# Two chunks of the second sequence take turns in layer one, and preparation work changes its place

## The chip, the core and the metric

The kernel runs on one core of one Trainium2 chip. The metric is device time in microseconds (us); lower is better. The core's engines run side by side, each with its own queue that it takes in order: TensorE (PE) multiplies matrices and loads their stationary side (PEld), VectorE (DVE), ScalarE (ACT) and GpSimd (POOL) do elementwise work, and SyncE (SP) issues the DMA transfers. Engines wait for each other by semaphores.

## The reference

Attention with a narrow window and block summaries, then two feed-forward parts, all in fp32:

```python
# 2 sequences, 8 heads, 768 positions, head size 64; block 32, window 16
k_sum = k.reshape(B, H, nb, block, D).max(axis=3)
v_sum = v.reshape(B, H, nb, block, D).mean(axis=3)
scores_l = where(|i - j| < 16, scale * q @ k.T, -1e9)
scores_s = scale * q @ k_sum.T + log(block)
attn = softmax(concat(scores_l, scores_s)) @ concat(v, v_sum)

x = attn as [1536 tokens, 512]
h = maximum(maximum(x @ w1, x @ w2), x @ w3)      # 512 -> 768
x = h @ w_out                                     # 768 -> 512
y = (x @ w_a) * (x @ w_b)                         # 512 -> 1536, twice
out = y @ w_out2                                  # 1536 -> 512
```

## The kernel before

**Work.** The 1536 tokens are four chunks of 384: chunks 0 and 1 are the first sequence, 2 and 3 the second. Attention goes by groups, one pair of heads in one chunk: eight groups per sequence, groups 0 to 3 for its first chunk and 4 to 7 for its second. A group has scores on PE (`ps`, L187), an exponential on ACT (L191), the reciprocal of the sum on DVE (`r`, L199), the normalization on POOL (`s`, L201), transposes on PE (`pst`, copied to `aT`), value products on PE (`psv`) and a split into two parts that gives `x`. `steps` (L233) is the generator that hands this out in 44 steps per sequence.

**Layers.** Every dense product is three matmuls on split operands (`mm3`, L362). `layers12(c)` (L374) is a generator of 22 turns for chunk `c`: 18 turns of layer one (`ph`, 12 matmuls each; the three weight sets are joined by a maximum on evacuation, then split into `hg`) and 4 turns of layer two (`py`, 18 matmuls each). Layer three (`layer3`, L461; PSUM tiles `qb`, `qg`, `qd`) multiplies by `w_a` and `w_b` with Strassen's seven products for each sequence; its operands `yt` are splits of sums and differences (`yd`) of the layer-two results, made by `sums_of` (L424). Layer four is `po` (L520).

**Weights.** All 60 weight tiles of 512 KB lie in HBM as 64-bit numbers. Each is loaded (`w_load`), rounded to fp32 on ACT, DVE and POOL (`w_round`, L300 to L306) and split (`w_split`, `w_parts`, L310 and L311). The first 24 (N12) serve layers one and two, the other 36 layers three and four. `weights(most)` (L335) moves the three stages on, if buffers have room by its count and, from weight 24 on, once `gate` has been set.

**Order.** SP's queue keeps the program's order. On the other engines a scheduler orders by its own estimate of when operations are ready; `tc.issue_after(ins)` forces what the block traces on the engine of `ins` behind `ins` in that engine's queue. `last[0]` is the last group's reciprocal (DVE), `mark[0]` the latest evacuation by DVE in layer one. The bottom of the program (L559 to L583) first walks through the first attention's steps and calls `weights` at some of them (`PRE`), then goes through the string `turns`, a digit per turn that names the chunk, with the second attention's steps strewn in between the turns that `TURNS` names, and at last through layers three and four.

## Time and profile before

| | before |
|---|---|
| time, median of 3 runs | 590.12 us (588.95 to 592.65) |
| the profiled execution: time, span | 591.21 us, 589.3 us |
| PE busy | 551.3 us (94%) |
| DVE busy | 377.8 us (64%) |
| ACT busy | 278.7 us (47%) |
| POOL busy | 208.2 us (35%) |
| TensorE clock granted, mean | 0.982 |

The profile is one execution. The span runs from its first instruction to its last; the profiled execution's own time is 1.9 us longer. Busy is the time in which an engine has an instruction; matmuls overlap one another, so a busy PE need not be at its full pace. [...] The chain of work that ended last is 63% PE, 14% DVE, 7% DMA, 5% POOL and 5% ACT.

### The profile page before, as it was taken

What the parts mean: (1) busy time and instruction counts of PE and PEld (TensorE: products, weight loads), DVE (VectorE), ACT (ScalarE), POOL (GpSimd) and SP (SyncE); (2) the same over time, 40 slices, a digit from 0 to 9 for tenths busy, and PEclk for the clock granted to TensorE, in tenths of its full rate; (3) what the DMA queues carried; (4) which work ended last, traced back from release to release, by engine and by line L of the source; (5) the groups of instructions that cost most, each with busy time, mean ns of one, the idle gap of its engine ahead of it and who ended that gap; (6) DMA issues with size and microseconds to landing.
All of it is one profiled execution on the core that took longest, in us unless ns stands there. A gap on an engine that the chain in (4) does not pass through costs nothing.

```text
span 589.3 us, 8831 instructions
## 1 busy us (share of the span) xinstructions
PE 551.3 (94%) x3272; PEld 513.3 (87%) x3272; DVE 377.8 (64%) x780; ACT 278.7 (47%) x667; POOL 208.2 (35%) x184
## 2 busy tenths in 40 slices
PE   4778999999999999998889899999999999999997
PEld 3567989999999999997888789999999989999985
DVE  4786398857213331249998775777696796883374
ACT  3777657444434332246675565653543544331220
POOL 0497269943001221035652433332341351330030
PEclk9959999999999999999999999999999999999999
DMA  9998035933211000052121123122212212000005
GB/s 265 344 273 247 36 110 190 298 73 107 63 47 48 1 1 1 1 222 85 52 72 43 66 72 108 37 72 72 71 41 77 98 37 72 2 1 0 1 17 198
DMA packets 31291, 53.32 MB, mean 90 GB/s; under 512 B 2448, under 2 KB 18832, under 8 KB 31248
## 3 DMA queue, kind: packets, MB, share of 16 engines
q1 hardware_dynamic: 31248, 52.75, 28.2%
q8 instruction: 26, 0.43, 0.3%
q14 instruction: 17, 0.14, 0.1%
HBM read 49.59 MB, written 3.15 MB: 89 GB/s over the span
## 4 chain that ended last, share of the span: by engine, by line
PE 63%; DVE 14%; DMA 7%; issue 5%; POOL 5%; ACT 5%; SPq 1%; POOLq 0%; ACTq 0%; DVEq 0%
PE ph L365 15%; PE qb L365 13%; PE py L365 7%; PE qg L365 5%; PE po L529 5%; DMA w<-wall 5%; PE po L527 5%; PE po L528 5%; POOL w L306 3%; DVE wt L311 3%; PE qd L365 3%; PE ps L187 2%; PE psv L228 2%; DVE hg L369 2%; DVE w L305 2%
## 5 line engine op out<-in xcount | busy, mean ns | idle before, releaser
L365 PE MATMUL ph<-x,wt 128*128 128x384 f32 x864 | 164.2, 343 | 3.8 <-DVE nm L190 2.0
L365 PEld LDWEIGHTS ph<-x,wt 128*128 128x128 f32 x864 | 150.7, 191 | 5.3 <-ACT wt L310 2.2
L306 POOL TENSOR_TENSOR w<-w,w 128x512 int32<-128x512 int32 x60 | 86.7, 1450 | 122.6 <-DVE w L305 73.5
L365 PE MATMUL qb<-yt,wt 128*128 128x384 f32 x576 | 114.2, 339 | 7.3 <-DVE t L496 2.0
L365 PEld LDWEIGHTS qb<-yt,wt 128*128 128x128 f32 x576 | 101.6, 188 | 14.0 <-DVE t L496 3.2
L368 ACT ACTIVATE hg<-t 128x384 fp32r<-128x384 f32 x72 | 36.9, 521 | 81.0 <-DVE t L392 36.0
L499 POOL TENSOR_TENSOR t<-t,ca 128x384 f32<-128x384 f32 x36 | 42.8, 1204 | 88.4 <-DVE t L498 85.7
L365 PE MATMUL qg<-yt,wt 128*128 128x384 f32 x288 | 59.4, 339 | 1.4 <-DVE t L498 0.6
L539 DVE TENSOR_TENSOR acc<-po,acc 128x512 f32<-128x512 f32 x60 | 40.8, 687 | 26.9 <-PE po L529 26.7
L527 PE MATMUL po<-wt,hg 128*128 128x512 f32 x144 | 56.4, 392 | 0.5 <-ACT hg L368 0.5
L528 PE MATMUL po<-wt,hg 128*128 128x512 f32 x144 | 56.5, 393 | 0.0
L529 PE MATMUL po<-wt,hg 128*128 128x512 f32 x144 | 55.8, 395 | 0.2 <-DVE hg L369 0.2
L365 PE MATMUL py<-hg,wt 128*128 128x384 f32 x288 | 55.1, 341 | 0.3 <-ACT hg L368 0.3
L365 PEld LDWEIGHTS qg<-yt,wt 128*128 128x128 f32 x288 | 50.9, 189 | 4.1 <-DVE t L498 0.9
L191 ACT ACTIVATE s<-s,nm 128x120 f32<-128x120 f32 x96 | 37.1, 388 | 33.3 <-DVE nm L190 32.9
L365 PEld LDWEIGHTS py<-hg,wt 128*128 128x128 f32 x288 | 49.6, 188 | 0.8 <-ACT hg L368 0.6
L392 DVE TENSOR_TENSOR t<-ph,t 128x384 f32<-128x384 f32 x48 | 26.3, 552 | 36.0 <-PE ph L365 31.6
L369 POOL TENSOR_TENSOR hg<-t,hg 128x384 fp32r<-128x384 f32 x24 | 26.8, 1116 | 61.8 <-ACT hg L368 61.8
L187 PE MATMUL ps<-kept,q 128*128 128x120 f32 x192 | 38.3, 319 | 10.6 <-DVE kept L133 7.7
L311 DVE TENSOR_TENSOR wt<-w,wt 128x512 fp32r<-128x512 f32 (+1 forms) x44 | 35.2, 799 | 20.0 <-ACT wt L310 20.0
L190 DVE CUSTOM_DVE_ANT_0 s<-ps,kept 128x120 f32<-128x120 f32 x96 | 24.6, 278 | 36.0 <-PE ps L187 35.4
L310 ACT ACTIVATE wt<-w 128x512 fp32r<-128x512 f32 (+1 forms) x60 | 35.0, 583 | 25.0 <-POOL w L306 12.6
(72 smaller groups left out, 789.1 us busy)
## 6 DMA issues: line engine op xcount, KB each, us to landing
w<-wall SPq DMA_DIRECT2D x60, 512.0 KB, 3.4
q<-qt SPq DMA_DIRECT2D x16, 384.0 KB, 7.2
kept<-kt SPq DMA_DIRECT2D x8, 448.0 KB, 6.9
full<-vt SPq DMA_DIRECT2D x8, 384.0 KB, 6.2
out<-acc SPq DMA_DIRECT2D x12, 256.0 KB, 2.0
v<-vwin SPq DMA_DIRECT2D x16, 144.0 KB, 5.4
v<-vwin SPq DMA_DIRECT2D x16, 96.0 KB, 5.7
v<-vwin SPq DMA_DIRECT2D x16, 48.0 KB, 6.7
```

What stands on the lines that cost most here:

```text
L187: T.matmul(ps[:, a], q[:, i, a], k_t[p][:, k0:k0 + NC], start=True, stop=True)
L191: A.activation(s[:, a], s[:, a], AF.Exp, bias=nm[:, a:a + 1], scale=-1.0, accum_out=sm[:, a:a + 1])
L306: G.tensor_tensor(w.bitcast(I32), w.bitcast(I32), lw.bitcast(I32), ALU.add)
L311: eng.tensor_tensor(w[:, 1], r, w[:, 0], ALU.subtract)
L365: T.matmul(ps, w[:, i, o:o + P], x[:, j], start=first and n == 0, stop=last and n == 2, skip_group_check=more)
L368: A.activation(dst[:, 0], src, AF.Copy)
L369: eng.tensor_tensor(dst[:, 1], src, dst[:, 0], ALU.subtract)
L499: G.tensor_tensor(t, t, cs[c, f], ALU.mult)
L527: T.matmul(ps, g[:, 0], w[:, 0], start=(f == 0), stop=False)
L528: T.matmul(ps, g[:, 0], w[:, 1], start=False, stop=False)
L529: T.matmul(ps, g[:, 1], w[:, 0], start=False, stop=(f == 1))
L539: V.tensor_tensor(acc[c, i], ps, acc[c, i], ALU.add)
```

## The change

- `PRE` goes from (9, 4) to (18, 5): in the first attention `weights` is called at step 18 and every fifth after it, where it was at step 12 and every fourth; six weights instead of eight are started there. On DVE these are queued behind a group's reciprocal.
- `turns` was six turns of chunk 0, twelve pairs of chunks 0 and 1, six of chunk 1, four of layer two each, then all 22 of chunk 2 and all 22 of chunk 3. The first 44 stay. Then come eight turns of chunk 2, ten pairs of chunks 2 and 3, the four layer-two turns of chunk 2 and the last twelve of chunk 3.
- The second attention's steps go into turns 20 to 44 (were: 24 to 60).
- `gate` is set by chunk 2's fourth `hg` tile (was: chunk 3's second), and `fits` lets the later weights start once chunk 3 has done nine turns of layer one (was: fifteen), with ten tiles at most as before. From chunk 2 on one weight is started per turn (was: two), behind the latest evacuations on DVE and on ACT.
- The first sequence's sums are traced at turns 58, 62, 66 and 70, behind those evacuations. They were traced at chunk 3's layer two and held back by one-element POOL copies that read `hg`; those copies are gone.
- The first six of the later weights are rounded through PSUM, as the first 24 are.

```diff
@@ -55,7 +55,11 @@
 W64, W32, WBUFS, QB, SM, GB, BANKS = (6, 3), (4, 3), (24, 10), 3, 2, (12, 9), (2, 2, 1, 2, 2)
-AHEAD, PRE, TURNS = (4, 1), (9, 4), (6, (24, 42), (42, 60))
+GATE, ROOM, SUMS, EARLY34 = (2, 3), 16, (58, 62, 66, 70), 6
+AHEAD, PRE, TURNS = (4, 1), (18, 5), ((6, N1 - 6, 6, 4, 4, 8, N1 - 8, 4, 12), (20, 32), (32, 44))
@@ -291,7 +295,7 @@
         r = w64_t.pop(q).bitcast(U32).rearrange("p (n t) -> p n t", t=2)
         lw, hw = r[:, :, 0], r[:, :, 1]
         to = hw.bitcast(F32)
-        if q < N12:
+        if q < N12 + EARLY34:
             to = ps_c.tile([P, 512], F32, tag="c", name="psw")
         if BIAS_DVE[era(q)][q % 3]:
@@ -332,11 +336,15 @@
     w_at, w_done, w_freed, w_room = [0, 0, 0], 0, 0, 0
+    def fits(n):
+        return n <= N12 or n - w_freed <= ROOM and n - max(N12, w_freed) <= WBUFS[1]
     def weights(most):
         nonlocal w_done, w_room
         for _ in range(most):
-            if w_done == len(seq) or w_room + room[w_done] > w_freed + WBUFS[w_done >= N12] or w_done == N12 and not gate:
+            if w_done == len(seq) or not fits(w_room + room[w_done]) or w_done == N12 and not gate:
                 return
             w_room += room[w_done]
             w_done += 1
@@ -369,7 +377,7 @@
         eng.tensor_tensor(dst[:, 1], src, dst[:, 0], ALU.subtract)
-    ys, gate, mark = {}, [], [None]
+    ys, gate, mark = {}, [], [None, None]
     def layers12(c):
@@ -387,12 +395,12 @@
             def evac(f=f, m=m, ps=ps, ht=hs[f]):
                 prev, pend[0] = pend[0], temp(f"t{m}", c)
                 if m == 0:
-                    A.activation(pend[0], ps, AF.Copy)
+                    mark[1] = A.activation(pend[0], ps, AF.Copy).ins
                 else:
                     mark[0] = V.tensor_tensor(pend[0], ps, prev, ALU.max).ins
                     if m == 2:
                         split(ht, pend[0], G)
-                        if lastc and f == 1:
+                        if c == GATE[0] and f == GATE[1]:
                             gate.append(ht[:, 0, 0:1])
             late.append(evac)
@@ -400,8 +408,6 @@
             yield
         ys[c] = y_p.tile([P, 4, MAXT * P], F32, tag="y", name="y", bufs=NCH)
         for m in range(4):
-            if lastc:
-                sums_of(m // 2, m % 2 * 2 + 1, [hs[f][:, 0, 0:1] for f in (2, 3, 4, 5)])
             ps = bank("py")[:, 0:n_]
             for f in range(N2):
                 if m == 0 and f == N2 - 1:
@@ -421,23 +427,18 @@
         if c >= 2 and m % 2:
             sums_of(c, m)
-    def sums_of(c, m, behind=None):
+    def sums_of(c, m):
         b, j = divmod(c, 2)
         (b11, b21), (b12, b22) = ((y[:, 0:2], y[:, 2:4]) for y in (ys[2 * b], ys[2 * b + j]))
         def op(name, src):
             ops[b, name] = t = t_p.tile([P, 2, 2, MAXT * P], F32R, tag=name, name="yt")
-            if behind is not None:
-                G.tensor_copy(t[:, 0, 0, 0:1], behind[m])
             A.activation(t[:, 0], src, AF.Copy)
             V.tensor_tensor(t[:, 1], src, t[:, 0], ALU.subtract)
         def diff(tag, x, y):
             t = y_p.tile([P, 2, MAXT * P], F32, tag=tag, name="yd")
-            if behind is not None:
-                G.tensor_copy(t[:, 0, 0:1], behind[m])
             V.tensor_tensor(t, x, y, ALU.subtract)
             return t
@@ -556,20 +557,33 @@
             q += 2
-    for i in range(2):
-        V.memset(vpad[i], 0.0)
+    for x in vpad:
+        V.memset(x, 0.0)
     for n, _ in enumerate(steps(0)):
-        weights(1 if n >= PRE[0] and n % PRE[1] == 0 else 0)
-    turns = TURNS[0] * "0" + (N1 - TURNS[0]) * "01" + TURNS[0] * "1" + "00001111" + (N1 + 4) * "2" + (N1 + 4) * "3"
+        if n >= PRE[0] and (n - PRE[0]) % PRE[1] == 0:
+            with tc.issue_after(behind):
+                weights(1)
+        else:
+            behind = last[0]
+    turns = "".join(x * y for x, y in zip(TURNS[0], ("0", "01", "1", "0", "1", "2", "23", "2", "3")))
     behind = last[0]
     dense, todo, done = [layers12(c) for c in range(NCH)], steps(1), 0
     for i, c in enumerate(turns):
         next(dense[int(c)])
-        with tc.issue_after(behind):
-            weights(2 if c > "1" else 1)
+        if c < "2":
+            with tc.issue_after(behind):
+                weights(1)
+        if c > "1":
+            with tc.issue_after(mark[0]), tc.issue_after(mark[1]):
+                weights(1)
+                if i in SUMS:
+                    m = SUMS.index(i)
+                    sums_of(m // 2, m % 2 * 2 + 1)
         due = sum(min(1, max(0, i + 1 - i0) / (i1 - i0)) for i0, i1 in TURNS[1:])
         while done < int((STEPS * NP + 2) * due + 1e-6):
```

What the scheduler makes of it, at three places. The first is PE's queue at the end of the first attention (`ps`, `pst`, `psv` are scores, transposes and value products of groups 5 to 7; `ph` is layer one). Before:

```order
L365 MATMUL ph<-x,wt 128x384 x10
L211 MATMUL pst<-kept,s 120x128 x6
L187 MATMUL ps<-kept,q_107 128x120 x2
L365 MATMUL ph<-x,wt 128x384 x12
L228 MATMUL psv<-aT,v_111 64x64 x12
L211 MATMUL pst<-kept,s 120x128 x6
L365 MATMUL ph<-x,wt 128x384 x12
L228 MATMUL psv<-aT,v_112 64x64 x12
L365 MATMUL ph<-x,wt 128x384 x210
```

and with the change:

```order
L373 MATMUL ph<-x,wt 128x384 x11
L191 MATMUL ps<-kept,q_107 128x120 x2
L215 MATMUL pst<-kept,s 120x128 x6
L232 MATMUL psv<-aT,v_111 64x64 x12
L373 MATMUL ph<-x,wt 128x384
L215 MATMUL pst<-kept,s 120x128 x6
L373 MATMUL ph<-x,wt 128x384 x11
L232 MATMUL psv<-aT,v_112 64x64 x12
L373 MATMUL ph<-x,wt 128x384 x204
```

The first attention's last value products now stand behind 60 matmuls of layer one; before, they stood behind 114.

The second is ACT's queue in groups 2 and 3 (`s,sm` are exponentials; L300 and L302 or, with the change, L304 and L306 round a weight, L310 or L314 split it; `r` is the sum of group 2). Before, with the first weight's two operations and two exponentials just ahead of these rows:

```order
L368 ACTIVATE x<-psv 128x384
L302 ACTIVATE w_304<-w_304 128x512
L150 ACTIVATE v_111<-psvs 24x3x128 x2
L300 ACTIVATE psw<-w_306 128x512
L302 ACTIVATE w_306<-w_306 128x512
L191 ACTIVATE s,sm<-s,nm 128x120 x2
L310 ACTIVATE wt<-w_315 128x512
L302 ACTIVATE w_308<-w_308 128x512
L191 ACTIVATE s,sm<-s,nm 128x120 x2
L302 ACTIVATE w_310<-w_310 128x512
L300 ACTIVATE psw<-w_308 128x512
L191 ACTIVATE s,sm<-s,nm 128x120 x2
```

(the next row is `r`), and with the change, from the first weight on:

```order
L304 ACTIVATE psw<-w_385 128x512
L306 ACTIVATE w_385<-w_385 128x512
L195 ACTIVATE s,sm<-s,nm 128x120 x2
L306 ACTIVATE w_387<-w_387 128x512
L195 ACTIVATE s,sm<-s,nm 128x120 x2
L154 ACTIVATE v_111<-psvs 24x3x128 x2
L195 ACTIVATE s,sm<-s,nm 128x120 x2
L202 ACTIVATE r<-sm 128x6
L306 ACTIVATE w_389<-w_389 128x512
L195 ACTIVATE s,sm<-s,nm 128x120 x2
L306 ACTIVATE w_391<-w_391 128x512
L306 ACTIVATE w_393<-w_393 128x512
```

From the first weight to `r` nine weight operations stood in the queue; now three do, and the landing of the fifth weight (`w_393`) stands ahead of group 3's `r`. The sixth weight's first operation stands a few rows further on, ahead of group 4's exponentials. On POOL the normalizations of groups 2 and 3 now follow each other ahead of all weight work; before, six weight operations stood ahead of the first of them.

The third is DVE's queue where the later weights begin (`t` are evacuations of layer one, `w` and `wt` weights, `yd` and `yt` the first sequence's differences and splits). Before:

```order
L392 TENSOR_TENSOR t_2785<-ph,t_2769 128x384
L304 TENSOR_SCALAR w_2916<-w_2912 128x512
L329 TENSOR_TENSOR s<-w_2827,s 128x256
L311 TENSOR_TENSOR wt<-s,wt 128x512
L305 SCALAR_TENSOR_TENSOR w_2916<-w_2912,w_2916 128x512
L304 TENSOR_SCALAR w_3082<-w_3078 128x512
L441 TENSOR_TENSOR yd<-y 128x768
L305 SCALAR_TENSOR_TENSOR w_3082<-w_3078,w_3082 128x512
L311 TENSOR_TENSOR wt<-s,wt 128x512
```

and with the change, where the first two of these weights begin:

```order
L442 TENSOR_TENSOR yd<-y 128x768
L438 TENSOR_TENSOR yt<-yd,yt 128x768
L400 TENSOR_TENSOR t_2613<-ph,t_2578 128x384
L400 TENSOR_TENSOR t_2628<-ph,t_2598 128x384
L308 TENSOR_SCALAR w_2639<-psw 128x512
L308 TENSOR_SCALAR w_2646<-psw 128x512
L309 SCALAR_TENSOR_TENSOR w_2639<-psw,w_2639 128x512
L309 SCALAR_TENSOR_TENSOR w_2646<-psw,w_2646 128x512
L400 TENSOR_TENSOR t_2666<-ph,t_2613 128x384
L442 TENSOR_TENSOR yd<-y,yd 128x768
```

The first sequence's sums stood behind the first weights of layer three; now four of their eleven operations stand ahead of those weights and the rest among the first operations on them. The second sequence's first two splits (chunk 2's) now follow the first two weights, where they stood ahead of all.

## Rows read from the trace of the kernel before

**Rows 1.** Page, busy tenths of 40 slices of 14.7 us.
```profile
PE   4778999999999999998889899999999999999997
...
DVE  4786398857213331249998775777696796883374
```

**Rows 2.** Stretches: us, busy us (x instructions) per engine, granted clock, DMA share, GB/s.
```profile
0.00:60.00 60.00, 40.09 (x268) 33.20 (x268) 39.47 (x130) 40.21 (x126) 32.21 (x35) 0.86 0.93 283
60.00:120.00 60.00, 58.53 (x405) 56.68 (x402) 45.20 (x88) 36.22 (x86) 43.09 (x34) 1.00 0.54 158
120.00:195.00 75.00, 74.91 (x552) 72.38 (x551) 29.80 (x114) 30.87 (x108) 15.62 (x17) 1.00 0.21 60
195.00:255.00 60.00, 60.00 (x409) 58.62 (x409) 16.85 (x50) 17.06 (x48) 9.37 (x9) 1.00 0.00 1
255.00:345.00 90.00, 79.42 (x427) 74.73 (x427) 77.85 (x117) 53.74 (x100) 42.00 (x39) 0.98 0.26 94
345.00:570.00 225.00, 222.70 (x1152) 204.98 (x1151) 156.93 (x266) 98.63 (x198) 63.04 (x51) 1.00 0.14 47
```

**Rows 3.** Timeline of PE: start us, us, what, [idle before <-releaser].
```profile
30.30 0.69 PE L365 MATMUL ph<-x,wt 128*128 128x384 f32 x1 [2.05 <-DVE nm L190]
...
82.89 36.73 PE L365 MATMUL ph<-x,wt 128*128 128x384 f32 x210 [0.59 <-ACT x L368]
```

**Rows 4.** Waits of PE, 255 to 345 us: total us, times, longest us.
```profile
PE qd L365 <- DVE yt L435: 1.6, 1, 1.6
...
PE qb L365 <- ACT yt L434: 1.6, 2, 1.2
PE qd L365 <- ACT yt L434: 1.6, 1, 1.6
```

**Rows 5.** Groups of ACT, 15 to 60 us: busy us, mean ns | idle before, releaser.
```profile
L191 ACT ACTIVATE s<-s,nm 128x120 f32<-128x120 f32 x28 | 10.8, 388 | 0.3 <-DVE nm L190 0.2
L302 ACT ACTIVATE w<-w 128x512 int32<-128x512 uint32 x13 | 8.7, 668 | 4.5 <-DMA w<-wall 4.5
```

**Rows 6.** Timeline of SP's DMA issues.
```profile
17.31 3.97 SPq L286 DMA_DIRECT2D w<-wall  x5
```

**Rows 7.** Timeline of ACT, first weight and group 2's sum.
```profile
23.86 0.64 ACT L300 ACTIVATE psw<-w 128x512 f32<-128x512 f32 x1 [0.86 <-DMA w<-wall]
...
33.35 0.20 ACT L198 ACTIVATE r<-sm 128x6 f32<-128x6 f32 x1
```

**Rows 8.** Stretches of 15 us in the first attention, as rows 2.
```profile
15.00:30.00 15.00, 10.31 (x86) 8.78 (x86) 11.86 (x45) 11.80 (x37) 6.93 (x11) 0.96 1.07 344
30.00:45.00 15.00, 11.78 (x58) 9.65 (x59) 11.88 (x32) 11.84 (x35) 15.00 (x13) 0.50 0.90 262
45.00:60.00 15.00, 11.88 (x105) 10.03 (x103) 8.63 (x33) 11.24 (x38) 9.86 (x8) 0.97 0.84 264
```

**Rows 9.** Timeline of POOL: normalizations of groups 2, 4 and 7.
```profile
37.19 1.85 POOL L201 TENSOR_TENSOR s<-s,r 128x720 f32<-128x720 f32 x1
...
52.72 1.38 POOL L201 TENSOR_TENSOR s<-s,r 128x720 f32<-128x720 f32 x1
...
76.08 1.39 POOL L201 TENSOR_TENSOR s<-s,r 128x720 f32<-128x720 f32 x1 [4.22 <-DVE r L199]
```

**Rows 10.** Groups of DVE, 240 to 360 us, as rows 5.
```profile
L435 DVE TENSOR_TENSOR yt<-yd,yt 128x768 fp32r<-128x768 f32 x8 | 8.4, 1051 | 0.0
...
L441 DVE TENSOR_TENSOR yd<-y 128x768 f32<-128x768 f32 x4 | 4.5, 1120 | 1.2 <-POOL yd L440 1.2
```

**Rows 11.** Timeline: first load for layer three (SP), its first matmul (PE).
```profile
255.66 90.81 SPq L286 DMA_DIRECT2D w<-wall  x17
...
275.23 0.62 PE L365 MATMUL qb<-yt,wt 128*128 128x384 f32 x2 [1.17 <-ACT yt L434]
```

**Rows 12.** Waits of PE, 0 to 60 us.
```profile
PE pst L211 <- POOL s L201: 2.1, 2, 1.4
PE psv L228 <- ACT aT L215: 2.1, 2, 1.3
```

## The prediction

> **What bounds the kernel now.** I read the slices of the page first, then busy time by stage, then TensorE's own rows. In the slices [rows 1] TensorE (PE) is at 9 nearly everywhere, with two dents: the first 60 us, and a shallow one from about 255 to 345 us, where VectorE (DVE) stands at 9 in many slices instead. A busy PE overstates the work, because matmuls overlap: 210 in a row from 82.89 us took 36.73 us [rows 3], 0.1745 us each. So I count the matmuls of a stretch and multiply.
>
> From 120 to 255 us PE is busy 134.9 of 135 us, and from 345 to 570 us 222.7 of 225 [rows 2]: nothing to win there, and something to lose. From 255 to 345 us it ran 427 matmuls [rows 2]: 427 x 0.1745 = 74.5 us, and 0.3 more for six wider ones of layer 4, so 15.2 of 90 us are lost. DVE was busy 77.9 us in the same stretch, more than PE had work. PE stood idle there for 90 - 79.4 = 10.6 us; at least 4.8 of these ended with `yt`, the sums' operands, on DVE or ScalarE (ACT) [rows 4].
>
> In the first 60 us PE is idle for 20 us while DMA is at 0.93 of its time [rows 2]: attention inputs and the first weights come together. ACT takes its queue in order, and that holds both kinds of work; one weight operation alone (L302) found 4.5 us of weights that had not landed [rows 5].
>
> **The change: the start.** I measure it by one state: first attention complete, PE free for dense work. Before, this is at 82.9 us [rows 3] with 114 matmuls of layer one done. After, PE's queue has 60 at that place. The missing 54 cost 54 x 0.1745 = 9.4 us later. If the first attention ends at T, the start gains 82.9 - (T + 9.4) - S, with S a wait for the next weight.
>
> T goes group by group (a group is one pair of heads in one chunk; its normalization on POOL, `s`, is the mark I follow).
> - The first five weights are issued behind the last values of chunk 0 instead of ahead of them, 672 KB later. Before they were issued from 17.31 us [rows 6] and ACT had the first at 23.86 [rows 7]. At 262 to 344 GB/s [rows 8] 672 KB are 2.0 to 2.6 us, so the first lands at about 26.2, and the fifth at about 33.5 (512 KB are 1.5 to 2.0 us).
> - Between ACT's first weight and the sum `r` of group 2, three weight operations stand in its queue where nine stood. Six at about 0.6 us (0.668 less the overlap, [rows 5]) are 3.6 us; a split and two scores that now go ahead are 1.1 more; the first weight is 2.3 later. `r` goes from 33.35 [rows 7] to 31 or 32.
> - On POOL `s` of groups 2 and 3 now stand ahead of all weight work. Before, the first of them began at 37.19 [rows 9], after queued weight work. After: near 32, and near 34.6 for group 3, whose `r` stands behind the fifth weight's landing.
> - Group 4: ACT has the sixth weight ahead of its first score. Its 512 KB follow 672 KB of inputs, so it lands near 38. Sixteen ACT operations later (8 scores of 0.388 us, 8 others of 0.2 to 0.67, [rows 5], 7 us in all) `s` of group 4 starts near 45; before at 52.72 [rows 9].
> - Groups 5 to 7: before, `s` of group 7 came at 76.08 [rows 9], so 7.8 us a group. After, less weight work stands between, but each group has a weight's landing ahead of it on ACT, and 11 to 14 matmuls of layer one ahead of its transposes on PE. The floor is what ACT itself does in a group: six scores, three weight operations [rows 5] and some small ones, 4.5 us; with a tail of 3.5 us, T = 45 + 13.5 + 3.5 = 62. The ceiling is the old spacing and the old tail (76.08 to 82.89): 45 + 23.4 + 6.8 = 75.2, say T = 76. I take 5.6 us a group, since waits on weights get fewer but do not go, and 5 us for the tail: T = 67.
>
> The sixth weight's DVE work is queued behind the last reciprocal, so PE waits about S = 2 us for it. Gain: 82.9 - 76.4 - 2 = 4.5 us; bounds +9.5 (T = 62) and -4.5 (T = 76). From there layer one asks for a new weight every two turns (4.2 us), the pace that 60 to 120 us had, where PE was busy 58.5 of 60 us and POOL 43.1 [rows 2]: no further loss.
>
> **The change: the middle.** The second attention's steps go from turns 24 to 60 into turns 20 to 44. PE's own work is the same, and PE is what is full there. DVE's 29.8 and ACT's 30.9 of 75 us [rows 2] leave room for half as much again. Chunk 3's first turn now comes right behind the last value product, so PE waits once for a split, as it does for 0.59 us at 82.89 [rows 3]. I take 1 us lost, bounds 0 and 4.
>
> **The change: from layer one to layer three.** Two things leave the stretch that DVE fills. The first sequence's sums (7 splits and 4 differences of 1.05 to 1.12 us, [rows 10], 12 us of DVE) go to turns 58 to 70; DVE was busy 16.9 of 60 us there [rows 2], which hides them. Without that cover they cost what they cost now. The 11 one-element POOL copies go, for which DVE waited 1.2 us [rows 10]. And the next layers' weights are loaded from about turn 60 and worked from turn 69. Before, their first load was at 255.66 us and layer three's first matmul 19.6 us later, behind `yt` [rows 11]. Since chunks 2 and 3 take turns, chunk 2's layer two (4 turns of 3.1 us) lies between the first of these weights and the end of layer one. `mark` keeps evacuations ahead: DVE gets four weight operations (2.4 us) behind turn 68's evacuation, against 2.1 us a turn, so an evacuation slips by some 0.5 us; the second PSUM bank takes that.
>
> DVE then has 77.9 - 12 = 66 us of work for 74.8 of PE and is no longer the longer one. What stays: behind chunk 3's layer two come the second sequence's 4 splits and 3 differences, 7 x 1.05 = 7.4 us of DVE, with the first sequence's products as PE's cover; I take 2 us, and 2 of today's 5.8 us of other waits. So 4 of 15.2 us are left and 11 are won. Bounds: 4.8 (only the `yt` waits go) and 14 (1 us left).
>
> The six weights rounded through PSUM put one operand of DVE elsewhere, as the first 24 weights do now: 0, bounds 1 us either way. From 345 us on the queues read as before: 0.
>
> **Sum.** 591.2 (profiled execution) - 4.5 + 1 - 11 = 576.7 us. The median of the runs shown is 1.1 us below the profiled one, so 575.6, rounded to 576.
>
> **Rivals.**
> *A: the start gains nothing.* With fewer layer-one matmuls between its small ones, PE is sparser during the first attention. The granted clock was 0.50 (1.2 GHz) in 30 to 45 us [rows 8], after gaps such as 2.05 us before 30.30, and a matmul took 0.69 us then [rows 3]. If it stays there to the end of the attention, 60 matmuls take 10 us more, and they stand ahead of the transposes of groups 4 to 7: T = 76, which gives 576 + 9 = 585; half of it (T = 71) gives 580. For it: the stretch from 30 to 45 us. Against: in 45 to 60 us, with 105 instructions on PE, the clock was 0.97 [rows 8], and 60 matmuls of layer one in 20 us are no sparser. [...]
>
> *B: the wait only moves to layer three.* DVE's queue has the second sequence's first two splits ahead of the later weights, and the second of them needs the end of chunk 2's layer two, so DVE stands idle for some 7 us in a stretch where it is wanted. If all of that comes back to PE, 4 us are won instead of 11: 583. For it: DVE is in order. Against: PE has chunk 3's last eight turns (16.8 us) then, which need evacuations alone.
>
> *C: slower.* The second attention, pressed into turns 20 to 44, stalls PE at each of its 8 groups. A transposition's wait for POOL and a value product's for ACT took up to 1.4 and 1.3 us in the first attention [rows 12]. Both in every group make 21.6 us: 576 + 21 = 597. It decides from 20 / 8 = 2.5 us a group on. Against: in 120 to 255 us PE is idle for 0.1 us in all, with POOL busy 25 of 135 us [rows 2].
>
> *D: everything fits.* T = 62 and 1 us left: 576 - 5 - 3 = 568.
>
> **Chances.** Forecast (571 to 581) 0.52; A 0.18, half of it the milder one; B 0.15; C 0.04; D 0.11. About 1% is what a measurement of this kernel can tell from no change: below 584.2 or above 596.0 us. The forecast, D, the milder A and two thirds of B are faster: 0.82. The rest of A and B lies within 1%: 0.14. C is slower: 0.04. The range of 566 to 587 leaves out C and the ends of A and D.
>
> **What would show it.** Right: `s` of group 7 on POOL near 62 us and the long run of layer-one matmuls from about 67; `yd` and `yt` of the first sequence on DVE before layer one ends; no wait of PE over 1 us for `yt`; less than 9 for DVE in the slices of the transition. Wrong: landings of weights ahead of ACT's scores that cost more than a group's work; a clock of 0.50 past 55 us; waits of PE for `s`, `aT` or `hg` in the second attention; waits of PE for `wt` in layer three.

## The result, and the profile after

The changed kernel takes 586.38 us (median of 7 executions, 584.24 to 586.85) against 590.70 (7, 588.95 to 592.70) on the same chip: a ratio of 0.991, interval 0.990 to 0.993. It gained 4.3 us where 14 were forecast; the time lies inside the range, at its upper end. The profiled execution is the fastest of the seven: 584.24 us, span 582.5, against 591.2 for the profiled one of before.

The page of the changed kernel, busy tenths in slices of 14.6 us, against [rows 1]:

```profile
PE   4768899899999999989999799999999999999997
...
DVE  4647998854223323694988966767787796883274
```

PE's second dent is now two slices, an 8 at 248 to 262 us and a 7 at 320 to 335, and DVE stands at 9 in three slices between 248 and 335 us, as many as before, where the prediction had less than 9 as its sign. The stretches, columns as [rows 2]:

```profile
45.00:60.00 15.00, 12.57 (x121) 11.66 (x119) 11.01 (x41) 11.00 (x42) 8.19 (x7) 1.00 0.28 88
0.00:60.00 60.00, 40.99 (x326) 35.46 (x326) 35.74 (x138) 40.54 (x140) 23.26 (x29) 0.91 0.78 242
60.00:120.00 60.00, 55.92 (x362) 53.72 (x361) 52.43 (x96) 38.93 (x83) 53.66 (x45) 1.00 0.68 208
...
255.00:345.00 90.00, 83.44 (x453) 79.90 (x452) 70.27 (x103) 50.44 (x97) 29.02 (x21) 0.98 0.20 65
345.00:570.00 225.00, 222.19 (x1147) 204.28 (x1146) 159.98 (x272) 94.69 (x190) 64.81 (x52) 1.00 0.15 48
```

The first 60 us have a clock of 0.91 instead of 0.86, and behind 345 us PE is as busy as before (222.19 against 222.70 us). In 255 to 345 us PE ran 453 matmuls instead of 427. By the prediction's own count, 453 x 0.1745 and 1.0 for nineteen wider ones of layer four make 80.1 us, so 9.9 of 90 us are lost there: not 15.2 as before, but not 4 either. PE's waits in 200 to 345 us, against [rows 4]:

```profile
PE qb L373 <- DVE t L499: 2.9, 1, 2.9
PE qb L373 <- DVE t L497: 0.9, 1, 0.9
PE qg L373 <- DVE wt L315: 0.9, 1, 0.9
PE qb L373 <- ACT s L483: 0.8, 1, 0.8
PE qb L373 <- ACT u L483: 0.8, 1, 0.8
```

No `yt` is waited for any more. What is left comes in two places. The first is layer three's first products, which the change lets TensorE take in the middle of chunk 2's layer two. Timeline of PE:

```profile
256.64 0.44 PE L373 MATMUL qb<-yt,wt 128*128 128x384 f32 x1 [0.82 <-ACT s L483]
257.96 1.38 PE L373 MATMUL qg<-yt,wt 128*128 128x384 f32 x5 [0.88 <-DVE wt L315]
```

PE waits for an accumulator and for `wt` while 36 ready matmuls of layer two stand behind them. Behind these waits the granted clock, a share of full speed, fell to 0.50 in this execution (stretch 259 to 262 us). Five matmuls of 384 columns took from 259.14 to 260.74 us there, 0.320 us each, where 0.173 is the pace at 1.00; 0.320 us are 1.2 columns a ns, the prediction's 1.2 GHz if a column is a cycle. splits_pool and evac_first, below, have the same two waits and kept 1.00 there:

```profile
259.00:262.00 3.00, 3.00 (x11) 3.00 (x10) 1.80 (x3) 1.72 (x4) 0.00 (x0) 0.50 0.00 0
```

The second place is layer three itself, 312 to 336 us. Its longest wait on PE, and what DVE did meanwhile (timelines of PE, then DVE):

```profile
323.63 2.25 PE L373 MATMUL qb<-yt,wt 128*128 128x384 f32 x12
328.79 1.31 PE L373 MATMUL qb<-yt,wt 128*128 128x384 f32 x6 [2.91 <-DVE t L499]
```

```profile
323.32 1.24 DVE L330 TENSOR_TENSOR s<-w 128x256 f32<-128x256 f32 x1
324.48 1.24 DVE L332 TENSOR_TENSOR s<-w,w 128x256 f32<-128x256 f32 x1
325.65 0.41 DVE L331 TENSOR_TENSOR s<-s,w 128x256 f32<-128x256 f32 x1
325.98 0.68 DVE L315 TENSOR_TENSOR wt<-w,wt 128x512 fp32r<-128x512 f32 x1
...
328.19 0.54 DVE L499 TENSOR_TENSOR t<-qb,m 128x384 f32<-128x384 f32 x1
```

PE's last twelve matmuls ahead of that wait began at 323.63 us and ended at 325.88; DVE frees the bank from 328.19 on, after weight operations and two splits that PE did not wait for then. Before the change the same wait stood at 336.40 us (1.63 us). The start in the same kernel, on PE (the view ends at 90 us), then on POOL (groups 2, 4 and 7, as [rows 9]):

```profile
33.00 1.53 PE L215 MATMUL pst<-kept,s 128*120 128x128 f32 x6 [3.97 <-POOL s L205]
...
51.98 2.20 PE L373 MATMUL ph<-x,wt 128*128 128x384 f32 x11 [1.90 <-DVE wt L315]
...
69.05 21.19 PE L373 MATMUL ph<-x,wt 128*128 128x384 f32 x119
```

```profile
31.55 1.39 POOL L205 TENSOR_TENSOR s<-s,r 128x720 f32<-128x720 f32 x1 [4.63 <-DVE r L203]
...
45.08 1.39 POOL L205 TENSOR_TENSOR s<-s,r 128x720 f32<-128x720 f32 x1 [2.35 <-DVE r L203]
...
63.39 1.39 POOL L205 TENSOR_TENSOR s<-s,r 128x720 f32<-128x720 f32 x1
```

The first attention ends at 69.05 us with 60 matmuls of layer one behind it, in this execution.

To compare kernels by stretch I use one measure below, **PE's lost time**: from one matmul's start to the next, less the pace of its kind where nothing waits (0.173 us for 384 columns, 0.23 for 512, 0.03 to 0.11 for attention's), summed. Worked out from each profiled execution, in us:

| kernel | to 90 us | 90 to 135 | 135 to 240 | 240 to 345 | behind 345 | median us | ratio to before |
|---|---|---|---|---|---|---|---|
| before | 35.0 | 0.4 | 5.2 | 16.1 | 5.2 | 590.7 | 1 |
| changed | 30.6 | 2.5 | 5.6 | 10.8 | 5.4 | 586.4 | 0.991 |
| start_alone | 33.2 | 0.1 | 5.2 | 16.5 | 5.0 | 590.2 | 0.999 |
| sums_alone | 33.6 | 0.1 | 5.2 | 16.4 | 7.6 | 593.3 | 1.005 |
| before_evac | 35.6 | 0.4 | 5.2 | 17.3 | 3.7 | 591.5 | 1.000 |
| splits_pool | 35.2 | 1.3 | 5.8 | 9.4 | 4.9 | 585.9 | 0.992 |
| hold2 | 32.7 | 2.4 | 5.6 | 7.6 | 5.1 | 585.4 | 0.990 |
| evac_first | 32.6 | 4.9 | 5.9 | 9.1 | 3.1 | 584.2 | 0.987 |
| room10 | 34.0 | 1.2 | 5.6 | 11.5 | 5.6 | 586.7 | 0.992 |
| hold2_evac | 33.2 | 1.1 | 5.5 | 5.9 | 3.0 | 579.0 | 0.978 |
| attn24 | 33.0 | 0.1 | 5.2 | 5.9 | 2.9 | 576.6 | 0.975 |
| attn24_noevac | 33.3 | 0.1 | 5.2 | 7.7 | 4.6 | 580.6 | 0.982 |
| best_room10 | 32.7 | 0.1 | 5.2 | 10.3 | 3.1 | 582.1 | 0.984 |
| best_sums | 33.6 | 0.1 | 5.2 | 13.8 | 3.4 | 584.8 | 0.989 |
| best_turns | 33.9 | 0.1 | 4.6 | 6.1 | 3.1 | 577.1 | 0.975 |
| best_start_old | 34.3 | 0.1 | 5.2 | 5.8 | 2.9 | 578.3 | 0.977 |
| best_pre13 | 32.8 | 0.1 | 5.1 | 5.9 | 3.0 | 576.3 | 0.976 |
| best_early0 | 31.6 | 0.1 | 5.2 | 6.4 | 2.9 | 575.5 | 0.973 |
| best_early12 | 32.4 | 0.1 | 5.2 | 5.0 | 5.8 | 577.7 | 0.976 |

The first column lies between 30.6 and 35.2 us in the executions of the new start and between 33.6 and 35.6 in those of the old, so it is read over all of them. The second lies between 1.1 and 4.9 us in the six kernels that have the changed kernel's program there. The others repeat within some 0.5 us, the lower clock aside. That lower clock, 1.7 us each time (in the changed kernel 0.50 for 3.4 us, 258.7 to 262.1), is in the column 240 to 345 once for before, changed, start_alone, splits_pool, evac_first, room10, best_room10, attn24_noevac and best_early0, twice for sums_alone and before_evac, for 5.4 us in best_sums, and not at all for the others. Each ratio's interval is about 0.002 to 0.004 either way. Medians come from different chips, on which the kernel before took 590.7 to 591.7 us; each ratio is taken on one chip.

### The profile page after: what moved, and what is told of

It is laid out like the page before. It is cut to its first block, busy times and chain, and to the rows that moved or that the text cites. A ratio compares the mean times of both kernels' runs of the same rounds, so it can differ in the third digit from the quotient of the medians.

```text
span 582.5 us, 8859 instructions
## 1 busy us (share of the span) xinstructions
PE 546.3 (94%) x3272; PEld 511.5 (88%) x3272; DVE 378.9 (65%) x780; ACT 278.1 (48%) x667; POOL 200.4 (34%) x173
## 4 chain that ended last, share of the span: by engine, by line
PE 60%; DVE 17%; DMA 10%; ACT 6%; issue 3%; POOL 3%; SPq 1%; POOLq 0%; ACTq 0%; DVEq 0%
PE ph L373 24%; PE qb L373 8%; DMA w<-wall 8%; PE py L373 6%; PE qg L373 4%; DVE wt L315 4%; PE po L528 3%; PE po L529 3%; PE po L530 3%; PE ps L191 3%; DVE w L309 2%; POOL w L310 2%; DVE hg L377 2%; PE psv L232 2%; DVE w L308 2%
## 5 line engine op out<-in xcount | busy, mean ns | idle before, releaser
L373 PE MATMUL ph<-x,wt 128*128 128x384 f32 x864 | 160.3, 338 | 3.3 <-DVE wt L315 1.9
L373 PEld LDWEIGHTS ph<-x,wt 128*128 128x128 f32 x864 | 149.1, 188 | 4.7 <-DVE wt L315 2.2
L310 POOL TENSOR_TENSOR w<-w,w 128x512 int32<-128x512 int32 x60 | 83.0, 1387 | 147.3 <-DVE w L309 89.4
L373 PEld LDWEIGHTS qb<-yt,wt 128*128 128x128 f32 x576 | 102.4, 189 | 12.7 <-DVE t L497 3.8
L191 PE MATMUL ps<-kept,q 128*128 128x120 f32 x192 | 39.7, 318 | 13.1 <-DVE kept L137 7.7
L191 PEld LDWEIGHTS ps<-kept,q 128*128 128x128 f32 x192 | 32.4, 216 | 16.8 <-DVE kept L137 7.9
L314 ACT ACTIVATE wt<-w 128x512 fp32r<-128x512 f32 (+1 forms) x60 | 35.1, 584 | 21.3 <-PE qb L373 12.1
L315 DVE TENSOR_TENSOR wt<-w,wt 128x512 fp32r<-128x512 f32 (+1 forms) x44 | 32.9, 747 | 18.7 <-ACT wt L314 18.7
```

The lines of the kernel that those rows point to most:

```text
L191: T.matmul(ps[:, a], q[:, i, a], k_t[p][:, k0:k0 + NC], start=True, stop=True)
L310: G.tensor_tensor(w.bitcast(I32), w.bitcast(I32), lw.bitcast(I32), ALU.add)
L314: A.activation(w[:, 0], r, AF.Copy)
L315: eng.tensor_tensor(w[:, 1], r, w[:, 0], ALU.subtract)
L373: T.matmul(ps, w[:, i, o:o + P], x[:, j], start=first and n == 0, stop=last and n == 2, skip_group_check=more)
```

## The experiments

**The start alone: start_alone.** The kernel before, with the new `PRE` and its wait:

```diff
-        weights(1 if n >= PRE[0] and n % PRE[1] == 0 else 0)
+        if n >= PRE[0] and (n - PRE[0]) % PRE[1] == 0:
+            with tc.issue_after(behind):
+                weights(1)
+        else:
+            behind = last[0]
```

> The kernel before with one part of the change: the first weights start at step 18 behind the last reciprocal, every fifth step. Theory 1 (the start gains by itself what the changed kernel's trace shows: first attention complete at 69.05 us with 60 matmuls of layer one done, against 82.89 with 114): 13.84 - 54 x 0.1745 = 4.4, less one wait of about 0.4, so 590.7 - 4 = 586.5 us, `s` of the last group near 62 us. Rival (the later weights make layer one wait until the second attention, gain given back): 590 us or more, with waits of PE for `wt` of over 3 us in sum between 60 and 120 us.

Measured: 590.2 us, ratio 0.9987 (0.9967 to 1.0006). Neither held: the time is the rival's, but between 60 and 120 us PE waited only 0.9 us for `wt`, so nothing was given back, there was less to gain. Its first attention ended here (timeline of PE, to 90 us):

```profile
71.39 18.84 PE L365 MATMUL ph<-x,wt 128*128 128x384 f32 x105
```

Over the 14 profiled executions with this start the end lies between 69.05 and 73.41 us, median 71.4; over four with the old one between 81.48 and 83.52, median 82.6. 82.6 - 71.4 - 9.4 = 1.8 us.

**The sums alone: sums_alone.** The kernel before, `sums_of` called without `behind` at turns 70, 74, 78, 82 under `tc.issue_after(mark[0])`.

> The kernel before with one part of the change: the first sequence's sums go to turns 70, 74, 78 and 82, inside chunk 3's layer one, behind the evacuations, without the one-element copies on POOL; weights and turns as before. Theory 1 (the sums were 12 us of DVE on the path): the waits for `yt` between 273 and 298 us, 8 us in the pace of the matmuls, mostly go: 590.7 - 5 to 7 = 584 to 586 us. Theory 2 (DVE's whole work of the transition sets the end, and the later weights start at the same place as before): the wait turns into one for `wt`, 589 to 590.5 us.

Measured: 593.3 us, ratio 1.0054 (1.0033 to 1.0074): slower by half a per cent. Waits of PE, 255 to 345 us:

```profile
PE qb L365 <- ACT u L480: 2.6, 1, 2.6
PE qb L365 <- DVE t L496: 2.3, 1, 2.3
PE ph L365 <- DVE t L392: 2.2, 1, 2.2
```

The waits for `yt` are gone but for 0.2 us, and as much is waited for evacuations that stand behind weight operations. The `u` of the longest wait stood on ACT behind a weight for whose landing ACT had waited 8.18 us. The sums' place by itself moves the wait.

**Rival B's gap: splits_pool.**

```diff
-            V.tensor_tensor(t[:, 1], src, t[:, 0], ALU.subtract)
+            (G if c == 2 else V).tensor_tensor(t[:, 1], src, t[:, 0], ALU.subtract)
```

> The changed kernel; the two splits of chunk 2's layer two (`yt<-y`) go to POOL, which is idle from 257.4 to 273.7 us there. Theory B (they stand ahead of the later weights in DVE's queue, so the 8.3 us in which DVE was idle before 269.25 come back as PE's waits from 314 to 336 us): DVE's gap at 261 is filled with weight operations, 586.4 - 3 to 5 = 581.5 to 583.5 us. Theory C (the weights had no buffers then anyway, and the waits from 314 on are layer three's own, DVE work queued ahead of the operations that free a bank): 586 us, within 1 us.

Measured: 585.9 us, 0.9920 (0.9893 to 0.9947), the changed kernel's time. The gap on DVE is where B put it, in the changed kernel (timeline of DVE):

```profile
269.25 0.96 DVE L438 TENSOR_TENSOR yt<-y,yt 128x768 fp32r<-128x768 f32 x1 [8.30 <-ACT yt L437]
```

but to take the splits out of DVE's queue brings nothing: the waits for `u` and `t` behind 314 us (0.77 and 2.91 us) are the same. Nor does it fill the gap. DVE then stands behind the next evacuation in its queue, for which TensorE's layer one has to run first (timeline of DVE in splits_pool):

```profile
272.76 0.56 DVE L400 TENSOR_TENSOR t<-ph,t 128x384 f32<-128x384 f32 x1 [9.43 <-PE ph L373]
```

What a filled gap would bring was therefore not measured.

**The two places of waits: hold2, evac_first, hold2_evac, attn24_noevac, before_evac.** hold2 makes layer three's products issue behind the last matmul of chunk 2's layer two (`hold[0]`); evac_first makes the weights of layers three and four issue behind the last sum that frees a bank:

```diff
-                mm3(to, wt, o + k * P, ops[b, y][:, :, k], ...)
+                with tc.issue_after(hold[0]):
+                    mm3(to, wt, o + k * P, ops[b, y][:, :, k], ...)
```

```diff
-                        V.tensor_tensor(t, to, x, ALU.add)
+                        mark3[0] = V.tensor_tensor(t, to, x, ALU.add).ins
...
-        weights(2)
+        with tc.issue_after(mark3[0] or mark[0]): weights(2)
```

> The changed kernel; layer three's products stand on TensorE behind the last matmul of chunk 2's layer two instead of between them. Theory 1 (what was lost from 255 to 262 us, 2.1 us of waits for an accumulator and `wt` and 1.7 us of a clock at 0.5 behind them, goes for good, since PE has chunk 3's layer one to work on meanwhile): 586.4 - 3.5 = 583 us, clock at 1.0 there. Theory 2 (the products were a lead that layer three lives from; the wait comes back behind 300 us): 586 us or more, with more than the 5.3 us that PE loses between 312 and 336 us.

> The changed kernel; in layers three and four DVE's weight operations are issued behind the last sum that frees a bank (`t<-qb,m`, `t<-qg,u`). Theory C (the waits of 2.9, 0.9 and 0.8 us at 314 to 336 us come from DVE's order: the operation that frees a bank stands behind weight operations that nobody waits for yet): those waits go, 586.4 - 3 to 4 = 582.5 to 583.5 us. Theory D (DVE has too much to do there in any order): the wait becomes one for `wt` or `hg`, 586 to 588 us.

> The changed kernel with both edits: layer three's products behind chunk 2's layer two, and weight operations behind the sums that free a bank. If the two losses are independent (the products' wait and lower clock at 255 to 262 us, of which the edit alone gave 1 us, and 3 to 4 us of waits from 314 on): 586.4 - 4 to 5 = 581.5 to 582.5 us. If DVE's throughput bounds the whole transition: 585 us.

Measured: 585.4 (0.9898, 0.9870 to 0.9926), 584.2 (0.9869, 0.9844 to 0.9895) and 579.0 us (0.9778, 0.9751 to 0.9805). One edit gives 1 to 2 us, both 7.4; hold2 by itself cannot be told from the changed kernel. Held, TensorE works through 255 to 262 us but for 0.6 us, and the wait for `t` stays (waits of hold2 in 240 to 345 us; line numbers are its own):

```profile
PE qb L373 <- DVE t L502: 3.1, 1, 3.1
PE qb L373 <- DVE t L500: 0.9, 1, 0.9
```

evac_first alone takes these down to 0.7 and 0.4 us, for a new wait of 1.6 us for ACT's `m`, and leaves those for `wt` (0.9), `s` and `u` (0.8 each):

```profile
PE qg L373 <- ACT m L483: 1.6, 1, 1.6
...
PE qb L373 <- DVE t L499: 0.7, 1, 0.7
PE qb L373 <- DVE t L497: 0.4, 1, 0.4
```

With both, the wait for `m` stays and those for `t` are 0.6 and 0.4 us:

```profile
PE qg L373 <- ACT m L486: 1.6, 1, 1.6
PE qb L373 <- DVE t L502: 0.6, 1, 0.6
...
PE qb L373 <- DVE t L500: 0.4, 1, 0.4
```

> As attn24, without the edit that puts weight operations behind the sums that free a bank. Theory 1 (both edits belong together: with the products held, TensorE meets DVE's queue order in layer three without a lead): 576.6 + 5 to 7 = 581.5 to 583.5 us, with the waits of 3.1 and 0.9 us for `t` back between 312 and 336 us. Theory 2 (the edits are independent, and this one is worth what evac_first measured): 576.6 + 2.6 = 579.2 us.

attn24_noevac took 580.6 us (0.9818, 0.9785 to 0.9851): beside held products DVE's order is worth 4 us, between the two theories and within the intervals of either, and its wait of 3.2 us is back.

> The kernel before with one edit that the change does not have: in layers three and four DVE's weight operations are issued behind the last sum that frees a bank. Theory 1 (layer three's own waits, 1.6 and 0.9 us at 334 to 342 us, are DVE's order alone and were there before the change): 590.7 - 2 to 3 = 588 us. Theory 2 (before, DVE has no slack in the transition, so weights pushed back come late): 591 us or more.

before_evac took 591.5 us (0.9996, 0.9973 to 1.0019): theory 2's time. Its waits for `t` are shorter, 0.7 and 0.4 instead of 1.6 and 0.9 us, and PE waits for ACT's `m` (2.8 us) and `ca` (2.3) instead. That this is DVE's want of slack, busy 77.85 of 90 us before the change, fits, but is not shown.

**The second attention's turns: attn24.** hold2_evac with

```diff
-(20, 32), (32, 44))
+(24, 34), (34, 44))
```

> As hold2_evac, with the second attention from turn 24 instead of 20 (to 44 as in the changed kernel). Theory: its first scores wait 1.6 to 1.8 us at 109 us for DVE, which is busy 52.4 of 60 us there with layer one's weights; four turns later these are done, so 1.5 us below hold2_evac. Rival: the steps, closer together, wait later instead (0.9 us each 15 us become 1.5): the same as hold2_evac within 0.7 us.

Measured: 576.6 us (0.9745, 0.9719 to 0.9770); the intervals overlap those of hold2_evac. The traces are clearer. In the changed kernel (timeline of PE):

```profile
111.36 0.70 PE L191 MATMUL ps<-kept,q 128*128 128x120 f32 x4 [1.61 <-DVE nm L194]
```

and in attn24, where the view begins at 100 us, 115 matmuls run through to the first of these scores:

```profile
99.79 20.10 PE L373 MATMUL ph<-x,wt 128*128 128x384 f32 x115
```

The loss from 90 to 135 us falls from 1.1 in hold2_evac to 0.1.

**What the mechanism is worth once the two waits are gone: room10, best_room10, best_sums, best_turns, best_start_old.** Each undoes one part of the change. room10 (on the changed kernel) and best_room10 (on attn24) set `ROOM` from 16 to 10, best_sums sets `SUMS` to `(78, 80, 82, 84)`, best_turns lets chunk 3 follow chunk 2, best_start_old takes the first weights' old place.

> The changed kernel, with the later weights' loads held until 15 of layer one's turns of chunk 3 are done, as before, where the change lets them begin at the ninth; sums, turns and start stay. Theory E (what the change gains in the transition comes from the weight work spread over 30 us more of DVE): the gain goes, 590 to 593 us, with PE's waits back between 270 and 300 us. Theory S (it comes from the sums' earlier place): 586.5 to 588 us.

> As attn24 (the changed kernel with the products held, the weight operations behind the bank-freeing sums, the second attention from turn 24), with the later weights held until 15 turns of chunk 3 as before the change. In the changed kernel itself that cost nothing (room10: 0.9915 against 0.9913). Theory 1 (there other waits hid it; with these gone the weights' lead counts): 576.6 + 4 to 6 = 580.5 to 582.5 us. Theory 2 (the lead is worth nothing): 576 to 577.5 us.

> As attn24, with the first sequence's sums at turns 78 to 84 (chunk 3's last turns of layer one and its layer two) instead of 58 to 70, the nearest place to that of before for which memory suffices. Theory 1 (the sums' 12 us of DVE must be done before the later weights' work; late, they push it onto TensorE's path): 576.6 + 4 to 8 = 580.5 to 584.5 us. Theory 2 (with the weights' lead and DVE's order mended, their place is free): 576 to 578 us.

> As attn24, but all of chunk 2's turns ahead of all of chunk 3's, as before the change; sums, weights and the other edits stay. Theory 1 (the alternation gives the lead between chunk 2's layer two and the end of layer one in which layer three's first products and weights fit): 576.6 + 4 to 6 = 580.5 to 582.5 us, the loss again between 270 and 300 us. Theory 2 (the sums' place alone carries it): 576 to 578 us.

> As attn24, with the first weights placed as before the change. Theory 1 (the new start gives what start_alone measured, since the first attention ends at 71.3 us with 60 matmuls where it ended at 81.4 with 114): 576.6 + 0.8 = 577.4 us, with first attention complete near 81 us. Theory 2 (the start's 4 us of the forecast were there, but given back in waits that the later edits have removed): 580 us.

Measured: room10 586.7 us, nothing; on attn24 the same edit costs 5.5 (582.1 us, 0.9843, 0.9809 to 0.9877), the late sums 8.2 (584.8 us, 0.9890, 0.9860 to 0.9921), the old start 1.7 (578.3 us, 0.9774, 0.9740 to 0.9809, at the edge of what can be told), the turns nothing (577.1 us, 0.9747, 0.9710 to 0.9783). The late weights and the late sums, waits of PE in 240 to 345 us of best_room10, then of best_sums:

```profile
PE qb L373 <- DVE ca L496: 3.3, 1, 3.3
```

```profile
PE qb L373 <- ACT u L486: 5.5, 1, 5.5
```

The wait for `u` in best_sums is not DVE's by itself, as its expectation had it. `u` stood on ACT behind a weight that had not landed, and that weight's load was issued only when POOL was done with a buffer (timelines of POOL, SP and ACT):

```profile
295.32 4.57 POOL L310 TENSOR_TENSOR w<-w,w 128x512 int32<-128x512 int32 x1 [4.83 <-DVE w L309]
```

```profile
299.91 0.33 SPq L290 DMA_DIRECT2D w<-wall  x1
```

```profile
303.26 0.66 ACT L304 ACTIVATE w<-w 128x512 f32<-128x512 f32 x1 [6.32 <-DMA w<-wall]
...
304.73 0.48 ACT L486 ACTIVATE u<-qb 128x384 f32<-128x384 f32 x1
```

POOL's operation took 4.57 us beside DVE's late sums, where the 60 of the changed kernel took 1.29 to 2.03, 1.31 at the median. Behind its wait best_sums also has a lower clock, 0.94 on the mean in 255 to 345 us where attn24 has 1.00: of the 13.8 us lost between 240 and 345 us, 90 x 0.06 = 5.4 are that clock. So the sums' place and the weights' lead carry the transition in attn24; the alternation of chunks 2 and 3 is not needed for it there.

**Smaller questions: best_pre13, best_early0, best_early12.** On attn24: the first weights at step 13, and none or twelve of the later weights rounded through PSUM instead of six.

> As attn24, with the first weights one group of the first attention earlier (step 13 instead of 18, then every fifth). Theory 1 (TensorE's 4 us wait for the third group's `s` and the lower clock behind it are what the start still loses; layer one's matmuls would fill them): first attention complete near 74 us with 72 matmuls or more of layer one, 1 us below attn24. Theory 2 (ScalarE's weight work delays the groups by as much): the same as attn24 within 1 us.

> As attn24, but none of the later weights is rounded through PSUM (six in the changed kernel). Theory 1 (in the changed kernel DVE's operations with both operands in SBUF take 0.4 to 1.2 us more beside a POOL operation and those with a PSUM operand do not; of 12 such operations some four would be slowed by 0.6 us, while DVE is the tight engine): 576.6 + 1 to 2 = 577.5 to 578.5 us. Theory 2 (the forecast's 0): 576.6 within 0.8 us.

> As attn24, with twelve of the later weights rounded through PSUM instead of six. Theory 1 (DVE's slowing beside POOL is part of what layer three's first groups lose): 576.6 - 1 = 575.5 us, 0.5 to 1 us less lost between 312 and 336 us. Theory 2: 576.6 within 0.8 us, or more where a PSUM bank of layer four is waited for.

Measured: 576.3 (0.9757, 0.9722 to 0.9792), 575.5 (0.9728, 0.9694 to 0.9762) and 577.7 us (0.9759, 0.9724 to 0.9795): none can be told from attn24. best_pre13's PE waits 6.7 us for the third group's `s` instead of 3.4, and its end is earned back by 13 more matmuls of layer one. The forecast's 0 for PSUM holds as far as can be told; best_early12 loses 0.9 us less than attn24 from 240 to 345 us and 2.9 more behind it.

## Why the prediction was wrong, point by point

- **The start, +4.5: mis-sized, T.** The steps held in the profiled execution of the changed kernel: first weight at 25.4 us (forecast 26.2), `s` of groups 2 and 4 at 31.55 and 45.08 us (forecast 32 and 45), the sixth weight's wait of 2 us there, but at 52 us, inside T. Group 7 came at 63.39 instead of 62, T = 69.05 instead of 67. That execution was the luckiest: the others have T = 70 to 73.4, with the first normalization up to 1.7 us later and `s` of group 7 18.3 to 20.9 us behind that of group 4 where 16.8 were set. The prediction's own terms for `r` of group 2 also give 33.35 - 3.6 + 1.1 + 2.3 = 33.15 us, not 31 or 32; over the 14 executions `s` behind it came between 31.55 and 34.42 us. With the median of 71.4 the term is 1.8 us, and the two kernels that change the start alone measured 0.8 (-0.4 to 1.9) and 1.7. A term read from one execution of before, on landings that shift by 2 us, was carried as if it were fixed.
- **The middle, -1: lost about 2.** Between 90 and 135 us 2.5 us are lost instead of 0.4, inside the bounds; five other profiles of the same program there lose 1.1 to 4.9. "DVE's 29.8 of 75 us leave room" was read from 120 to 195 us; the pressed attention begins at 109 us, where DVE is busy 52.4 of 60.
- **The transition, +11: the step that failed.** The `yt` waits went, as forecast. But "DVE is no longer the longer one", and with it "2 of today's 5.8 us of other waits", was argued from a sum of work. DVE's work did fall, from 77.85 to 70.27 us, where 66 was forecast. The other waits did not, since those for DVE come from its order: operations that free a bank stand behind weight operations in layer three, 2.9 + 0.9 us, and evac_first, which changes this order alone, brings them to 0.7 + 0.4. The 0.8 us for ACT's `u` is not of this kind; evac_first leaves it. And a wait that the prediction named among those that would prove it wrong, PE's for `wt` in layer three, came at 256 to 258 us, with 1.7 us of a lower clock behind it in this execution. Together they gave back half of what the lead had won: 10.8 of 16.1 us are still lost. With both removed 5.9 are, and then the sums' place is worth 8.2 us and the weights' lead 5.5, so the mechanism was there. For the lead, room10 beside best_room10 shows that the two waits hid it; the late sums were tried on attn24 alone.
- **The turns.** The prediction let chunk 2's layer two give the lead. best_turns shows, on attn24, that the lead comes from `ROOM` and `SUMS`, not from the alternation.
- **Behind 345 us, 0: right** (5.2 and 5.4). evac_first shows 2 us to be won there.
- **The sum.** With the start's 1.8 us by medians, and the table's -2.1 for the middle, -0.4 for 135 to 240 us, +5.3 for the transition and -0.2 behind it, 4.4 us come out; 4.3 were measured. All but the first are read from one pair of profiles, so the agreement is in part luck.
- **Rival A** did not happen: the clock was back at 1.00 in 45 to 60 us in the changed kernel's profile. In nine of the 14 executions with this start it fell again for 3 us or more, behind the sixth weight's wait. In these nine `s` of group 7 came 19.6 to 20.9 us behind that of group 4, in the other five 18.3; yet the median of T is 71.4 in both, since the start itself shifts as much. That T is near the milder A's 71, with a clock that was low for some 3 us and not to the middle of the attention. **Rival B's** place and size were right (8.3 us of idle DVE). Its price stays open: splits_pool took the splits away and the gap remained. **C** did not happen, **D** neither.

attn24, at 576.6 us, beats both kernels and takes the forecast's time, by two edits more than the forecast thought needed and later turns of the second attention.

**Open.** Why the two edits give 7.4 us together and 1 and 2.1 apart is explained only in part. In the traces they add up: behind 240 us (the last two columns) the changed kernel loses 16.2 us, hold2 12.7, evac_first 12.2 and hold2_evac 8.9, so 3.5, 4.0 and 7.3 us less; and evac_first's edit is worth 3.5 us from attn24_noevac to attn24. So in the traces the order is worth about the same with and without held products. Some 1.7 us of what the hold saves is the lower clock, which is not in each execution. The medians of the single edits fall short of that; ahead of 135 us, where the six kernels have one program, their profiles lose 33.1 to 37.5 us, which is as large as the effects.

## What to carry to other kernels

When an in-order engine is near its limit, count not only its work in a stretch but what stands ahead of the instruction that frees a bank or feeds the next one: less work brought half of what it promised here until evacuations stood ahead of preparation. When a scheduler is given earlier operands it will use them: look which ready work the first consumer then stands in front of. A term read from the start of a kernel, where landings shift from one execution to the next, needs several executions, and the median of the times says more than one pair of profiles.

## What the runs showed of the hardware

Behind a wait of 2 us the granted clock fell to 0.50 in some executions and stayed at 1.00 in others. In hold2 PE waited 1.90 us for the sixth weight, and then ran at 0.50 for 3 us (stretches):

```profile
50.00:53.00 3.00, 1.10 (x7) 0.85 (x6) 2.90 (x8) 1.57 (x6) 1.39 (x1) 0.95 0.18 72
53.00:56.00 3.00, 3.00 (x12) 3.00 (x11) 0.78 (x2) 0.41 (x3) 1.30 (x1) 0.50 0.00 0
```

Nine of the 14 executions with this start show this; start_alone, attn24 and the changed kernel have the same wait and no fall there (changed kernel: 1.00 in 50 to 53 and in 53 to 56 us). What decides between the two is not shown. Where it fell, another 1.7 us were lost to the clock behind a wait of 2 us.

In the changed kernel some operations of DVE with both operands in SBUF took longer beside POOL: `s<-w` took 0.43 us at 302.15, with POOL idle, and 1.24 at 323.32, during two POOL products (322.80 to 325.44); `wt<-s,wt` took 0.69 us at 317.77, with POOL idle, and 1.09 at 322.30. `t<-ph,t`, with one operand in PSUM, took 0.54 to 0.56 us in both cases (14 instructions, 225 to 345 us). What makes the difference is not shown. In best_sums POOL's own operation was the longer one, 4.57 us beside DVE's `yd` and `yt`. By way of the weights' rounding all this decides nothing that can be told: best_early0 and best_early12 change how many of DVE's operations can be slowed so, and took 575.5 and 577.7 us beside attn24's 576.6.
